# Converting the output projection's weights later, beside the gated block of batch 0, and spreading the other weight conversions over more of the attention

## The chip, the cores and the metric

The program runs on one core of a Trainium2 chip. The metric is the device time of one execution in microseconds (us). A core has five instruction streams: PE (matrix products), DVE and ACT (elementwise work and copies out of the accumulators), POOL (elementwise, slower), and SP, which here only issues DMA transfers. ACT issues DMA transfers too. Each stream runs its instructions strictly in its written order.

## The reference

Three stages, in float32 accuracy; batch 2, 8 heads, 768 positions, 64 values per head:

```python
# 1 attention, only between positions whose 6 hash bits agree
mask   = bucket(q @ proj) == bucket(k @ proj)
attn   = softmax(where(mask, q @ k.T / 8, -1e9));   x = attn @ v      # x: [2, 768, 512]
# 2 gated block ("MoE")
h = relu(x @ w_in);  u, v = h[..., :512], h[..., 512:]
v = w_spatial @ layernorm(v) + b_spatial            # mixes positions
x = (u * v) @ w_out
# 3 channel MLP
x = x + relu(layernorm(x) * g @ w_ch1) @ w_ch2      # 512 -> 2048 -> 512
```

The weights `w_in` (halves u and v, 512x512 each), `w_out` (512x512), `w_ch1` and `w_ch2` arrive as float64 values, that is as pairs of 32-bit words.

## The kernel before

**Products.** Each float32 operand is split into a high part of few bits and the remainder (`split_hi`, `split_lo`), and a product is three passes (high by high, high by low, low by high) of matrix instructions. So each weight tile exists as two halves, "hi" and "lo".

**Stages.** Attention runs in 96 steps: 2 batches x 8 heads x 2 groups x 3 query tiles of 128 rows (`attn_step`, line 876). A step makes scores (`sc`), their masked maximum (`x <- sc`, DVE), the exponentials (`x <- x`, ACT), their transposes on PE (`pt`), the copies of these out of the accumulators (`e <- pt`, shared between DVE and ACT), and once per head the product with v (`po`). Names carry batch, head, group and tile: `sc_1_2_0_1` is batch 1, head 2, group 0, tile 1. From step 60 (`M0`) on, the gated block of batch 0 (`moe1`, line 1007) is mixed in between the steps; that of batch 1 follows the attention, and the channel MLP follows it. In the gated block `pv_b_t_1` is the product of position tile t with the weight's v half, `pv_b_t_0` with its u half; `xT <- pv` (ACT) is the relu of the u half, `vr <- pv` (ACT) that of the v half; `act_x` is the split input, `vn` the normalized v, `w_sp` the split spatial weight.

**Converting a weight piece.** `conversions` (line 973) lists twelve pieces, four each of `out`, `v`, `u`. A piece has four parts (`converted`, line 942): a load of 512 KB of 64-bit words issued on ACT (`f64_*`), one ACT operation and five DVE operations on the two words (`f64c_*`), a join on POOL, and the split (hi by ACT, lo by POOL) into the weight tile. Once a whole weight is converted, it is stored to DRAM in one DMA of 2 MB issued on ACT (`kept`, line 966; `ws_out`, `ws_v`, `ws_u`); the copies that batch 1 needs, and `w_out` for both batches, are loaded back later by SP. `CONV_AT` (line 521) gives the attention step of each piece, and `CONV_D` the steps by which its parts stand off. `w_out` is converted first, in the buffer that later holds the normalized v (tag "vn"). The pieces of `w_ch1` and `w_ch2` (`f64_w1_*`, `f64_w2_*`) are converted in the same way in the later stages. The buffers of the loaded words and of the conversion's results are rings of two.

**What sets the order.** The kernel first records all operations as jobs (class `Plan`, line 170), so that every instruction carries line 494 in the profile. A list scheduler (`run`, line 296) then writes each engine's order: with modelled durations it takes, on the engine that is free first, the ready job with the earliest due time. Due times come from a pass backwards (`latest`, line 397); the two alternate and the best order is kept (`settle`). `opened` (line 317) holds a job back: until the matrix work recorded 60 jobs earlier has started, and until 20 us (`EARLY`) before its due time. So a changed place, size or buffer of one job may move instructions of every engine, also in stages that the change doesn't touch.

**SP's work in the attention.** For each head SP loads `k`, `q`, `v` and moves the split pieces into place: `qs <- q`, `ks <- k` and the mask rows `qs <- m`, `ks <- m`. The scores of a head wait for these.

Of the kernel before, what the change touches and what calls it, by code (L numbers as in the profile page):

```python
# [9 lines left out]
F32 = mybir.dt.float32  # L10
F32R = mybir.dt.float32r
# [7 lines left out]
P = 128  # L19
# [10 lines left out]
class View:  # L30


    def __init__(self, base, steps, box, dims, dtype):
        self.base, self.steps, self.box, self.dims, self.dtype = base, steps, box, dims, dtype
# [125 lines left out]
def cells(x):  # L160

    if isinstance(x, View):
        return x.columns
    n = 1
    for d in x.shape[1:]:
        n *= d
    return n


class Plan:  # L170
# [14 lines left out]
    RATE = {"load": 300e3, "move": 195e3, "store": 200e3}  # L185

    def __init__(self, tc):
        self.tc, self.jobs, self.pools, self.part, self.behind = tc, [], [], 0, None
        for name, key in (("tensor", "PE"), ("vector", "DVE"), ("scalar", "ACT"), ("gpsimd", "POOL"), ("sync", "SP")):
            setattr(self, name, Engine(self, key))  # L190

    def add(self, engine, op, args, kw):
        writes = [kw["out"] if "out" in kw else args[0]]
        rest = [*(args if "out" in kw else args[1:]), *(x for k, x in kw.items() if k not in ("out", "accum_out"))]
        if "accum_out" in kw:
            writes.append(kw["accum_out"])
        reads = [x for x in rest if isinstance(x, View)]
        views = [(x, True) for x in writes if isinstance(x, View)] + [(x, False) for x in reads]
        prev = self.jobs[-1] if self.jobs else None
        if (  # L200
            engine == "PE"
            and prev is not None
            and prev.engine == "PE"
            and prev.part == self.part
            and not prev.closed
            and prev.out is writes[0].base
            and prev.kind == (op, cells(writes[0]), writes[0].rows)
            and len(prev.calls) < (12 if cells(writes[0]) == 384 and op == "matmul" and reads[0].dtype == F32 else self.RUN)
        ):
            job = prev  # L210
        else:
            job = Job(len(self.jobs), engine, self.part)
            self.jobs.append(job)
            if engine == "PE":
                job.out, job.kind = writes[0].base, (op, cells(writes[0]), writes[0].rows)
        if self.behind:
            job.after.add(self.behind)
        busy, lag = self.cost(engine, op, writes, [x for x in rest if hasattr(x, "dtype")], kw, job)
        job.calls.append((op, args, kw))
        job.busy, job.lag = job.busy + busy, lag  # L220
        for x, w in views:
            for j, box, w2 in x.base.uses:
                if (w or w2) and j is not job and all(a < d and c < b for (a, b), (c, d) in zip(box, x.place)):
                    job.after.add(j)
            x.base.uses.append((job, x.place, w))
        return None
# [69 lines left out]
    def run(self, late=None):  # L296
# [12 lines left out]
        parts = {e: {} for e in engines}  # L309
# [5 lines left out]
        reached, when = [-1], [0.0]  # L315

        def opened(j):
            i = bisect_left(reached, j.at - self.LOOK)
            if i == len(reached):
                return None  # L320
            bulk = self.BULK if j.engine == "ACT" and j.bytes > 200000 else 0.0
            return max(when[i], bulk, late[j] - self.EARLY) if late else max(when[i], bulk)

        def done(j):
            stack = [j]
# [22 lines left out]
        while todo:  # L348
# [21 lines left out]
            j = min((j for j in c if ready[j] <= t + 1e-9), key=rank)  # L370
# [129 lines left out]
def attn_moe_kernel(ctx: ExitStack, tc: tile.TileContext, qT, kT, v, proj, w_in, w_spT, b_sp, w_out, g_ln, w1, w2, out):  # L500
# [3 lines left out]
    nc = plan = Plan(tc)  # L504
# [4 lines left out]
    w_in, w_out, w1, w2 = (  # L509
        w.bitcast(U32).rearrange("(k p) (f t) -> p k f t", p=P, t=2) for w in (w_in, w_out, w1, w2)  # L510
    )
    HF = DFF // 2
    DFF2 = w1.shape[2]
    NQT = S // P
    NKT = S // P
# [2 lines left out]
    CB0 = 2  # L518
    VB = (((0, 1, 2), (3, 4, 5)), ((0, 1), (2, 3, 4), (5,)))
    CB = 2  # L520
    CONV_AT = (5, 9, 14, 19, 24, 29, 34, 39, 44, 49, 53, 57)
    CONV_D = (-1, 0, 3, 3)
    QA = 3
    QB = 2
# [15 lines left out]
    KFT = DM // P  # L540
# [9 lines left out]
    def split_hi_v(dst, src):  # L550
        nc.scalar.activation(dst, src, AF.Copy)
# [4 lines left out]
    def split_lo(dst, src, hi):  # L556
        nc.gpsimd.tensor_tensor(dst, src, hi.bitcast(F32), op=ALU.subtract)
# [3 lines left out]
    def stage_f64(src, nm):  # L561
        a, n = src.shape[1], src.shape[2]
        st = pools["conv"].tile([P, a, n, 2], U32, tag="f64", name=f"f64_{nm}")
        nc.scalar.dma_start(out=st, in_=src)
        return st

    def words_f64(st, nm):

        a, n = st.shape[1], st.shape[2]
        lo, hi = st[:, :, :, 0], st[:, :, :, 1]  # L570
        c = pools["conv"].tile([P, a, n], U32, tag="f64c", name=f"f64c_{nm}")
        cf = c.bitcast(F32)
        nc.scalar.activation(cf, hi.bitcast(F32), AF.Abs)
        nc.vector.tensor_scalar(cf, cf, F64_MIN, F64_MAX, op0=ALU.max, op1=ALU.min)
        nc.vector.tensor_scalar(c, c, 3, 0x3FFFFFFF, op0=ALU.logical_shift_left, op1=ALU.bitwise_and)
        nc.vector.scalar_tensor_tensor(hi, hi, 0xC0000000, c, op0=ALU.bitwise_and, op1=ALU.bitwise_or)
        nc.vector.tensor_scalar(c, hi, 0xFF800000, None, op0=ALU.bitwise_and)
        nc.vector.scalar_tensor_tensor(cf, lo, 2.0**-52, cf, op0=ALU.mult, op1=ALU.mult)
        return hi.bitcast(F32), cf

    def join_f64(tf, cf):
        nc.gpsimd.tensor_tensor(cf, tf, cf, op=ALU.add)
        return cf

    def split_f64(dst_hi, dst_lo, tf):
        split_hi_v(dst_hi, tf)
        split_lo(dst_lo, tf, dst_hi)
# [20 lines left out]
    for a, own in enumerate((slice(0, D), slice(D, P))):  # L608
        for i, sign in enumerate((1.0, -1.0, 1.0)):
            at = a * HROW + i * NB  # L610
# [17 lines left out]
    dram = Pool(plan, "dram", space=bass.MemoryType.DRAM)  # L628
# [21 lines left out]
    mp = Pool(plan, "mp", 2, side="right", till=2)  # L650
# [287 lines left out]
    w_split = {}  # L938
    wp = {}
    moe_w = []  # L940

    def converted(src, dst, nm, after=None):

        d = {}

        def stage():
            d["st"] = stage_f64(src, nm)

        def words():
            d["tc"] = words_f64(d["st"], nm)  # L950

        def join():
            d["f"] = join_f64(*d["tc"])

        def finish():
            to = dst()
            split_f64(to[:, 0], to[:, 1], d["f"])
            if after:
                after(to)

        return stage, words, join, finish

    def kept(key, shape, to):
        w_split[key] = dram.tile(shape, F32, tag=f"ws_{key}", name=f"ws_{key}")
        nc.scalar.dma_start(out=w_split[key], in_=to.bitcast(F32))

    def moe_tile(key, b):
        pool = mp if len(moe_w) % 2 else keep
        wp[key, b] = pool.tile([P, 2, KFT, HF], F32R, tag="w", name=f"w_{key}_{b}", bufs=1)
        moe_w.append(wp[key, b])  # L970
        return wp[key, b]

    def conversions():

        res = []
        for key, src, at in (("out", w_out, 0), ("v", w_in, HF), ("u", w_in, 0)):
            for k in range(KFT):

                def dst(key=key, k=k):
                    if k == 0:  # L980
                        if key == "out":
                            wp[key] = mp.tile([P, 2, NKT, HF], F32R, tag="vn", name="w_out", bufs=1)
                        else:
                            wp[key] = moe_tile(key, 0)
                    return wp[key][:, :, k : k + 1]

                def after(to, key=key):
                    kept(key, [P, 2, KFT, HF], wp.pop(key)[:, :, :KFT])

                src_k = src[:, k : k + 1, at : at + HF]  # L990
                res.append(converted(src_k, dst, f"{key}_{k}", after if k == KFT - 1 else None))
        return res

    def reload(key, b):
# [148 lines left out]
    for _ in range(WARM2):  # L1143
        nc.tensor.transpose(warm, ident, ident)
    head_prep3(0, 0)
    convs = conversions()
    conv_steps = {}
    for at, stages in zip(CONV_AT, convs):
        for delay, e in zip(CONV_D, stages):
# [3 lines left out]
    for i in range(-1 - QA, NT + PO + 3):  # L1153
        attn_step(i)
        for e in pair_steps.get(i, ()):
            e()
        if i == 2:
            nc.sync.dma_start(out=b_sb, in_=b_sp.rearrange("(n p) -> p n", p=P))
        for e in conv_steps.get(i, ()):
            e()  # L1160
        if i == M0:
            m0 = moe1(0, ps_b, "b")
        if m0 is not None:
            while n0 < (i - M0 + 1) * 24 / (NT - M0):
                next(m0, None)
                n0 += 1
# [199 lines left out]
```

## Time and profile before

| | us |
|---|---|
| three runs | 665.03, 667.38, 668.51 |
| median | 667.38 |
| the profiled execution | 669.14 |
| its span on the core | 666.8 |
| PE busy in it | 651.5 |
| DVE, ACT, POOL busy | 430.3, 302.1, 198.3 |
| chain of work that ended last: PE, DVE, DMA | 87%, 7%, 3% |
| 2 MB stores issued on ACT at | 163.35 (w_out), 198.86 (w_v), 267.2 (w_u) |

"Busy" is the time in which an engine had an instruction running, out of the stretch named. Matrix instructions overlap each other and their ends are modelled, so that PE can read 100% and still run closer or wider. "Idle before" with an arrow names the instruction that ended a wait. A start is counted from the span's start. The attention of batch 0 and the beginning of batch 1 fill 10 to 155 us; the gated block of batch 0 lies beside the rest of the attention up to about 300; the gated block of batch 1 and the channel MLP follow.

### The profile page before, as it was taken

The page shows a single profiled execution, that of the slowest core. Times are in us where ns is not written, and L with a number is a line of the kernel's source. Part 1 is how long each engine was busy: PE and PEld are TensorE (multiplying, and loading weights), DVE is VectorE, ACT ScalarE, POOL GpSimd, SP SyncE. Part 2 cuts the span into 40 slices and gives each one's busy share as a digit, 9 for nine tenths or more (in the row PEclk, how much of TensorE's full clock was granted, in tenths as well). Part 3 has the DMA queues.
Part 4 walks back from the last instruction along what each step waited for, and adds up shares of the span by engine and source line. Part 5 has one row for each costly group of instructions (what it writes and reads, how often), then busy time and mean ns, then how long its engine had stood idle before and what let it go on. Part 6 is the DMA issues. An engine that isn't in the chain of part 4 may idle for free.

```text
span 666.8 us, 9374 instructions
## 1 busy us (share of the span) xinstructions
PE 651.5 (98%) x3376; PEld 510.2 (77%) x3376; DVE 430.3 (65%) x804; ACT 302.1 (45%) x581; POOL 198.3 (30%) x184
## 2 busy tenths in 40 slices
PE   7999999989999999999899999999999999999997
PEld 5776767767777777877688888888888888888886
DVE  5699779998657544443899695788862358622122
ACT  5788877776556545433364343432321133311110
POOL 2234424446325311100324433054450044510000
PEclk8999999999999999999899999999999999999999
DMA  6776775755539442906343441722210222200031
GB/s 167 187 190 168 190 162 154 220 134 179 146 97 336 102 105 71 327 27 227 129 151 121 144 132 47 284 95 87 84 51 1 64 85 87 81 1 16 1 111 63
DMA packets 47413, 83.72 MB, mean 126 GB/s; under 512 B 5676, under 2 KB 32136, under 8 KB 46344
## 3 DMA queue, kind: packets, MB, share of 16 engines
q1 hardware_dynamic: 34104, 53.64, 28.3%
q10 hardware_dynamic: 13264, 29.50, 13.2%
q8 instruction: 27, 0.44, 0.3%
q14 instruction: 18, 0.15, 0.1%
HBM read 51.42 MB, written 12.58 MB: 96 GB/s over the span
## 4 chain that ended last, share of the span: by engine, by line
PE 87%; DVE 7%; DMA 3%; issue 1%; ACT 1%; POOL 0%; SPq 0%; ACTq 0%; DVEq 0%; POOLq 0%
PE pc L494 20%; PE acc L494 20%; PE pv L494 8%; PE po L494 8%; PE sc L494 8%; PE pg L494 8%; PE pt L494 7%; PE py L494 5%; DVE x L494 2%; DMA f_w<-in_w 1%; DVE f64c_u L494 1%; PE pm L494 1%; PE ptr_g L494 1%; PE px_c L494 1%; DMA qs<-m 1%
## 5 line engine op out<-in xcount | busy, mean ns | idle before, releaser
L494 PE MATMUL acc<-w2t,ch 128*128 128x512 f32 x576 | 141.8, 393 | 0.0
L494 PE MATMUL pc<-xh,w1t 128*128 128x512 f32 x576 | 141.8, 394 | 0.0
L494 PEld LDWEIGHTS pc<-xh,w1t 128*128 128x128 f32 x576 | 108.0, 188 | 24.7
L494 PEld LDWEIGHTS acc<-w2t,ch 128*128 128x128 f32 x576 | 108.0, 188 | 24.5
L494 ACT ACTIVATE x<-x,nb 128x768 f32<-128x768 f32 x96 | 89.7, 935 | 29.9 <-DVE x L494 27.9
L494 DVE TENSOR_SCALAR_CACHE_REDUCE x<-sc 128x768 f32<-128x768 f32 x96 | 90.9, 952 | 17.8 <-PE sc L494 12.0
L494 DVE SCALAR_TENSOR_TENSOR ch<-pc,ch 128x512 fp32r<-128x512 f32 x48 | 33.1, 690 | 106.5 <-ACT ch L494 106.4
L494 PE MATMUL sc<-ks,qs 128*128 128x512 f32 (+3 forms) x384 | 94.9, 367 | 6.9 <-DVE x L494 3.6
L494 ACT ACTIVATE ch<-pc 128x512 fp32r<-128x512 f32 x48 | 28.7, 598 | 146.1 <-PE pc L494 146.0
L494 PE MATMUL pt<-ident,x 128*128 128x128 f32 x576 | 82.6, 276 | 0.9 <-DVE m L494 0.6
L494 PEld LDWEIGHTS sc<-ks,qs 128*128 128x128 f32 (+1 forms) x384 | 64.3, 194 | 21.7 <-DVE x L494 5.7
L494 POOL TENSOR_TENSOR f64c_w<-f_w,f64c_w 128x512 f32<-128x512 f32 x32 | 44.6, 1395 | 114.6 <-DVE f64c_w L494 95.0
L494 PEld LDWEIGHTS pt<-ident,x 128*128 128x128 f32 x576 | 68.0, 142 | 13.3 <-ACT e L494 4.1
L494 ACT ACTIVATE e<-pt 128x384 f32<-128x384 f32 x120 | 55.8, 484 | 26.5 <-PE pt L494 25.8
L494 PE MATMUL po<-e,vv 128*64 128x384 f32 x384 | 65.5, 490 | 0.0
L494 DVE COPY e<-pt 128x384 f32<-128x384 f32 x72 | 39.6, 552 | 17.9 <-PE pt L494 17.6
L494 PEld LDWEIGHTS po<-e,vv 128*64 128x64 f32 x384 | 26.2, 137 | 31.3 <-issue 30.1
L494 PE MATMUL pg<-vn,w_sp 128*128 128x512 f32 x180 | 45.0, 399 | 0.0
L494 PE MATMUL pv<-w_u,act_x 128*128 128x512 f32 x144 | 36.3, 400 | 2.3 <-ACT xT L494 2.2
L494 PEld LDWEIGHTS pg<-vn,w_sp 128*128 128x128 f32 x180 | 33.0, 188 | 7.1
L494 DVE TENSOR_SCALAR f64c_w<-f64c_w 128x512 f32<-128x512 f32 x64 | 32.6, 511 | 7.2 <-ACT f64c_w L494 6.5
L494 PE MATMUL pv<-w_v,act_x 128*128 128x512 f32 x144 | 37.1, 406 | 0.0
(132 smaller groups left out, 777.5 us busy)
## 6 DMA issues: line engine op xcount, KB each, us to landing
f_w<-in_w ACTq DMA_DIRECT2D x32, 512.0 KB
ks<-k SPq DMA_DIRECT2D x45, 192.0 KB
qs<-q SPq DMA_DIRECT2D x31, 192.0 KB
wst_sp<-in_w_spT SPq DMA_DIRECT2D x12, 384.0 KB
w_out<-ws_out SPq DMA_DIRECT2D x2, 2048.0 KB
vv<-in_v SPq DMA_DIRECT2D x16, 192.0 KB
ot<-y_dram SPq DMA_DIRECT2D x12, 256.0 KB
qs<-q SPq DMA_DIRECT2D x31, 96.0 KB
```

The source lines that it names most:

```text
L494: getattr(getattr(nc, engine[j.engine]), op)(*map(live, args), **{k: live(x) for k, x in kw.items()})
```

## The change

The order of the weights becomes v, u, out. The attention steps of the pieces become wider apart and later. A new flag `soon`, set while the conversions are recorded, takes their jobs out of the rule that holds a job until 20 us before its due time. The pieces of `w_out` no longer share the buffer "vn": hi and lo of a piece go into buffers of the spatial weight (tags `sp0`, two buffers, and `sp1`, one), and each is stored alone, 256 KB, so that `w_out` leaves in eight stores. `w_v` and `w_u` are still stored in one DMA of 2 MB each. No arithmetic is added or removed.

```diff
@@ -213,6 +213,7 @@
+        job.soon = self.soon
@@ -319,7 +320,7 @@
             if i == len(reached):
                 return None
             bulk = self.BULK if j.engine == "ACT" and j.bytes > 200000 else 0.0
-            return max(when[i], bulk, late[j] - self.EARLY) if late else max(when[i], bulk)
+            return max(when[i], bulk, late[j] - self.EARLY) if late and not j.soon else max(when[i], bulk)
 
         def done(j):
             stack = [j]
@@ -518,7 +519,7 @@
-    CONV_AT = (5, 9, 14, 19, 24, 29, 34, 39, 44, 49, 53, 57)
+    CONV_AT = (5, 11, 18, 24, 31, 37, 44, 50, 58, 62, 66, 70)
@@ -954,15 +955,10 @@
 
         def finish():
             to = dst()
-            split_f64(to[:, 0], to[:, 1], d["f"])
-            if after:
-                after(to)
+            split_f64(to[0], to[1], d["f"].rearrange("p a n -> p (a n)"))
+            after(to)
 
         return stage, words, join, finish
-
-    def kept(key, shape, to):
-        w_split[key] = dram.tile(shape, F32, tag=f"ws_{key}", name=f"ws_{key}")
-        nc.scalar.dma_start(out=w_split[key], in_=to.bitcast(F32))
 
     def moe_tile(key, b):
         pool = mp if len(moe_w) % 2 else keep
@@ -973,22 +969,29 @@
     def conversions():
 
         res = []
-        for key, src, at in (("out", w_out, 0), ("v", w_in, HF), ("u", w_in, 0)):
+        for key, src, at in (("v", w_in, HF), ("u", w_in, 0), ("out", w_out, 0)):
+            w_split[key] = dram.tile([P, 2, KFT, HF], F32, tag=f"ws_{key}", name=f"ws_{key}")
             for k in range(KFT):
 
                 def dst(key=key, k=k):
+                    if key == "out":
+                        parts = [
+                            mp.tile([P, NKT * P], F32R, tag=f"sp{i}", name=f"w_out_{k}_{i}", bufs=2 - i) for i in range(2)
+                        ]
+                        return [x[:, :HF] for x in parts]
                     if k == 0:
-                        if key == "out":
-                            wp[key] = mp.tile([P, 2, NKT, HF], F32R, tag="vn", name="w_out", bufs=1)
-                        else:
-                            wp[key] = moe_tile(key, 0)
-                    return wp[key][:, :, k : k + 1]
-
-                def after(to, key=key):
-                    kept(key, [P, 2, KFT, HF], wp.pop(key)[:, :, :KFT])
+                        wp[key] = moe_tile(key, 0)
+                    return [wp[key][:, i, k] for i in range(2)]
+
+                def after(to, key=key, k=k):
+                    if key == "out":
+                        for i in range(2):
+                            nc.scalar.dma_start(out=w_split[key][:, i, k], in_=to[i].bitcast(F32))
+                    elif k == KFT - 1:
+                        nc.scalar.dma_start(out=w_split[key], in_=wp.pop(key).bitcast(F32))
 
                 src_k = src[:, k : k + 1, at : at + HF]
-                res.append(converted(src_k, dst, f"{key}_{k}", after if k == KFT - 1 else None))
+                res.append(converted(src_k, dst, f"{key}_{k}", after))
         return res
 
     def reload(key, b):
@@ -1156,8 +1159,10 @@
             e()
         if i == 2:
             nc.sync.dma_start(out=b_sb, in_=b_sp.rearrange("(n p) -> p n", p=P))
+        plan.soon = True
         for e in conv_steps.get(i, ()):
             e()
+        plan.soon = False
         if i == M0:
             m0 = moe1(0, ps_b, "b")
         if m0 is not None:
```

The scheduler carries this further. Three places matter below. In each the name of an instruction is "written <- read".

First, ACT where the attention has ended and the gated block of batch 1 begins. Before (`f64_w1_1` is a load that ACT issues, `xT_1...<-pv_1_1_0` the relu of tile 1's u half):

```order
L494 DMA f64_w2_0_3576<-in_w2 128x1024
L494 ACTIVATE f64c_w1_0_3584<-f64_w1_0_3526 128x512
L494 ACTIVATE act_x1_3_3621<-xT_1_1858 128x512
L494 ACTIVATE xT_1_1858<-pv_1_0_0_3568 128x4x128
L494 ACTIVATE vr_1_2_3637<-pv_1_2_1_3569 128x512
L494 ACTIVATE f64c_w2_0_3640<-f64_w2_0_3576 128x512
L494 DMA f64_w1_1_3659<-in_w1 128x4x256
L494 ACTIVATE xT_1_1858<-pv_1_1_0_3627 128x4x128
L494 ACTIVATE act_x1_4_3665<-xT_1_1858 128x512
L494 ACTIVATE w1t_0_3678<-f64c_w1_0_3584 128x512
L494 ACTIVATE w_sp_early_3680<-wst_sp1_1_3578 128x768
```

Now:

```order
L495 ACTIVATE f64c_w1_0_3582<-f64_w1_0_3538 128x512
L495 ACTIVATE act_x1_3_3627<-xT_1_1842 128x512
L495 ACTIVATE xT_1_1842<-pv_1_0_0_3584 128x4x128
L495 DMA f64_w2_0_3635<-in_w2 128x1024
L495 ACTIVATE vr_1_2_3644<-pv_1_2_1_3585 128x512
L495 ACTIVATE w_sp_early_3663<-wst_sp1_1_3592 128x768
L495 ACTIVATE act_x1_4_3676<-xT_1_1842 128x512
L495 ACTIVATE xT_1_1842<-pv_1_1_0_3637 128x4x128
L495 ACTIVATE f64c_w2_0_3700<-f64_w2_0_3635 128x512
L495 ACTIVATE vn_1_3703<-vr_1_0_3568 128x512
L495 ACTIVATE xc_0_0_3536<-xc_0_0_3536,r0_c0_3666 128x512
L495 ACTIVATE vr_1_3_3716<-pv_1_3_1_3669 128x512
```

The load of `f64_w1_1` and the relu of `pv_1_1_0` have changed places: the load stood right ahead of the relu, and now it stands ten rows behind it, below the last row shown. The relu stands three rows behind `vr_1_2` in both, and `f64_w2_0`'s first ACT operation, which stood ahead of the relu, now stands behind it and ahead of `vr_1_3`.

Second, DVE around the first steps of head 1 of batch 1. Before (`f64c_u` and `f64_u` belong to the conversion of the u weight):

```order
L494 TENSOR_SCALAR f64c_u_1_1739<-f64c_u_1_1739 128x512
L494 TENSOR_SCALAR x_1_1_1_0_1838,nb_1_1_1_0_1837<-sc_1_1_1_0_1795 128x768
L494 COPY e_1_1_0_1798<-pt_1_1_0_0_1_1789 128x3x128
L494 TENSOR_SCALAR x_1_1_1_1_1847,nb_1_1_1_1_1846<-sc_1_1_1_1_1805 128x768
L494 TENSOR_SCALAR f64c_u_1_1739<-f64c_u_1_1739 128x512
L494 COPY e_1_1_0_1798<-pt_1_1_0_1_1_1818 128x3x128
L494 SCALAR_TENSOR_TENSOR f64_u_1_1665<-f64_u_1_1665,f64c_u_1_1739 128x512
L494 TENSOR_SCALAR f64c_u_2_1840<-f64c_u_2_1840 128x512
L494 COPY xT_1_1858<-po_1_0_1822 64x384
L494 TENSOR_SCALAR f64c_u_1_1739<-f64_u_1_1665 128x512
L494 TENSOR_SCALAR f64c_u_2_1840<-f64c_u_2_1840 128x512
L494 TENSOR_SCALAR x_1_1_1_2_1882,nb_1_1_1_2_1881<-sc_1_1_1_2_1860 128x768
```

Now:

```order
L495 TENSOR_SCALAR x_1_1_0_2_1781,nb_1_1_0_2_1780<-sc_1_1_0_2_1760 128x768
L495 SCALAR_TENSOR_TENSOR q2_1_1_1624<-q2_1_1_1624 128x768
L495 TENSOR_SCALAR x_1_1_1_0_1807,nb_1_1_1_0_1806<-sc_1_1_1_0_1785 128x768
L495 COPY e_1_1_0_1783<-pt_1_1_0_0_1_1776 128x3x128
L495 TENSOR_SCALAR x_1_1_1_1_1833,nb_1_1_1_1_1832<-sc_1_1_1_1_1803 128x768
L495 COPY e_1_1_0_1783<-pt_1_1_0_1_1_1798 128x3x128
L495 COPY xT_1_1842<-po_1_0_1813 64x384
L495 TENSOR_SCALAR x_1_1_1_2_1864,nb_1_1_1_2_1863<-sc_1_1_1_2_1845 128x768
L495 COPY e_1_1_0_1783<-pt_1_1_0_2_1_1851 128x3x128
L495 COPY e_1_1_1_1872<-pt_1_1_1_0_1_1866 128x3x128
L495 TENSOR_SCALAR x_1_2_0_0_1896,nb_1_2_0_0_1895<-sc_1_2_0_0_1878 128x768
```

The conversions of the u weight are gone from this place. They stand earlier; the pieces of `w_out` follow from head 2 of batch 1 on.

Third, ACT at the end of head 4 of batch 0. Before:

```order
L494 ACTIVATE e_0_4_0_901<-pt_0_4_0_2_0_961 128x3x128
L494 ACTIVATE e_0_4_1_995<-pt_0_4_1_0_0_982 128x3x128
L494 ACTIVATE e_0_4_1_995<-pt_0_4_1_0_1_988 128x3x128
L494 ACTIVATE x_0_4_1_2_993,z_sum_0_208<-x_0_4_1_2_993,nb_0_4_1_2_992 128x768
L494 ACTIVATE f64c_v_1_1028<-f64_v_1_958 128x512
```

Now:

```order
L495 ACTIVATE e_0_4_1_984<-pt_0_4_1_0_1_980 128x3x128
L495 ACTIVATE e_0_4_1_984<-pt_0_4_1_1_0_986 128x3x128
L495 DMA ws_v_1016<-w_v_0_599 128x4096
L495 ACTIVATE x_0_4_1_2_1011,z_sum_0_208<-x_0_4_1_2_1011,nb_0_4_1_2_1010 128x768
L495 ACTIVATE x_0_5_0_0_1031,z_sum_0_208<-x_0_5_0_0_1031,nb_0_5_0_0_1030 128x768
```

The 2 MB store of `w_v` has come here; before, it stood in batch 1, beside the gated block. In the same way that of `w_u` now stands ahead of the first exponential of batch 1's head 1.

## Rows read from the trace of the kernel before

**Rows 1.** First page: span, and PE's busy time.

```profile
span 666.8 us, 9374 instructions
...
PE 651.5 (98%) x3376; PEld 510.2 (77%) x3376; DVE 430.3 (65%) x804; ACT 302.1 (45%) x581; POOL 198.3 (30%) x184
```

**Rows 2.** Busy us by stretch: PE, PEld, DVE, ACT, POOL; PE clock; DMA; GB/s.

```profile
325.75:328.09 2.34, 0.16 (x1) 0.00 (x1) 2.34 (x4) 0.65 (x2) 2.23 (x2) 1.00 0.02 3
328.09:333.00 4.91, 4.91 (x15) 3.89 (x16) 3.79 (x9) 2.28 (x5) 1.70 (x2) 0.65 0.33 107
```

**Rows 3.** Timeline of POOL; start, us, instruction, idle before and releaser.

```profile
325.03 1.90 POOL L494 TENSOR_TENSOR f64c_w<-f_w,f64c_w 128x512 f32<-128x512 f32 x1 [3.80 <-DVE f64c_w L494]
```

**Rows 4.** Timeline of ACT at the same place.

```profile
326.95 0.39 ACTq L494 DMA_DIRECT2D f_w<-in_w  x1
327.44 0.60 ACT L494 ACTIVATE xT<-pv 128x512 f32<-128x512 f32 x1 [4.00 <-POOL f64c_w L494]
```

**Rows 5.** Timeline of PE at the same place.

```profile
328.09 1.75 PE L494 MATMUL pv<-w_u,act_x 128*128 128x512 f32 x6 [2.18 <-ACT xT L494]
```

**Rows 6.** Busy us by stretch over the attention, columns as in rows 2.

```profile
20.00:60.00 40.00, 39.06 (x268) 27.78 (x267) 35.13 (x71) 32.74 (x72) 14.33 (x14) 1.00 0.69 177
60.00:100.00 40.00, 39.37 (x266) 28.56 (x266) 32.49 (x71) 32.99 (x72) 14.81 (x15) 1.00 0.73 178
100.00:130.00 30.00, 29.25 (x199) 20.81 (x196) 27.72 (x56) 24.18 (x52) 12.53 (x13) 1.00 0.69 189
130.00:160.00 30.00, 28.24 (x185) 19.86 (x183) 29.81 (x56) 21.33 (x44) 15.75 (x15) 1.00 0.62 162
160.00:200.00 40.00, 39.66 (x227) 31.19 (x226) 24.37 (x54) 21.61 (x43) 15.03 (x14) 1.00 0.44 124
```

**Rows 7.** Timeline of DVE, the same form of instruction twice.

```profile
143.01 0.42 DVE L494 TENSOR_SCALAR f64c_u<-f64c_u 128x512 uint32<-128x512 uint32 x1
...
145.67 1.50 DVE L494 TENSOR_SCALAR f64c_u<-f64c_u 128x512 uint32<-128x512 uint32 x1
```

**Rows 8.** Timeline of POOL beside it.

```profile
145.50 2.80 POOL L494 TENSOR_TENSOR act_x<-xT,act_x 128x512 fp32r<-128x512 f32 x2 [4.91 <-ACT act_x L494]
```

**Rows 9.** Timeline of PE behind it.

```profile
148.23 0.98 PE L494 MATMUL sc<-ks,qs 128*128 128x512 f32 x4 [1.54 <-DVE x L494]
```

**Rows 10.** Waits of PE, 20 to 160 us: waited for, total, times, longest.

```profile
PE sc L494 <- DMA qs<-m: 0.7, 1, 0.7
```

**Rows 11.** Timeline of SP with no store beside it.

```profile
130.41 1.30 SPq L494 DMA_DIRECT2D qs<-q  x2
131.76 0.79 SPq L494 DMA_DIRECT2D qs<-m  x1
132.65 1.12 SPq L494 DMA_DIRECT2D ks<-k  x2
```

**Rows 12.** Timeline of SP right behind the store of w_out.

```profile
165.73 2.10 SPq L494 DMA_DIRECT2D qs<-q  x2
167.87 1.52 SPq L494 DMA_DIRECT2D qs<-m  x1
169.50 1.66 SPq L494 DMA_DIRECT2D ks<-k  x2
```

**Rows 13.** Instructions by form, DVE, 0 to 340 us: count, busy, mean ns.

```profile
L494 DVE SCALAR_TENSOR_TENSOR f64c_out<-f_out,f64c_out 128x512 f32<-128x512 uint32 x4 | 3.9, 963 | 0.1
...
L494 DVE TENSOR_SCALAR f64c_out<-f64c_out 128x512 uint32<-128x512 uint32 x4 | 2.9, 726 | 0.1
L494 DVE SCALAR_TENSOR_TENSOR f_out<-f_out,f64c_out 128x512 uint32<-128x512 uint32 x4 | 2.8, 692 | 0.0
...
L494 DVE TENSOR_SCALAR f64c_out<-f64c_out 128x512 f32<-128x512 f32 x4 | 1.9, 475 | 1.7 <-ACT f64c_out L494 1.7
...
L494 DVE TENSOR_SCALAR f64c_out<-f_out 128x512 uint32<-128x512 uint32 x4 | 1.7, 426 | 0.1
```

**Rows 14.** Timeline of DVE, the last two additions.

```profile
663.17 0.76 DVE L494 TENSOR_TENSOR ot<-acc,ot 128x256 f32<-128x256 f32 x2 [0.67 <-PE acc L494]
```

More of the change, by code (lines that the diff above doesn't have):

```diff
@@ L187, in __init__ @@
     def __init__(self, tc):
-        self.tc, self.jobs, self.pools, self.part, self.behind = tc, [], [], 0, None
+        self.tc, self.jobs, self.pools, self.part, self.behind, self.soon = tc, [], [], 0, None, False
         for name, key in (("tensor", "PE"), ("vector", "DVE"), ("scalar", "ACT"), ("gpsimd", "POOL"), ("sync", "SP")):
```

## The prediction

> **What bounds the kernel now.** The first page is read first: PE works 651.5 of 666.8 us [rows 1]. A change that leaves the arithmetic alone can only touch the other 15 us, or the spacing within. So the next view is busy time by stretch, to find where PE is not full. The reader is to see two places. One is the attention from 20 to 160 us, where PE stands idle 0.94, 0.63, 0.75 and 1.76 us in the four stretches, while DVE is busy 88, 81, 92 and 99% of them; from 160 to 200 us DVE falls to 61% and PE idles 0.34 us [rows 6]. So PE's small losses grow with DVE's load there. The other is the passage from attention to the gated block of batch 1, near 326 us. The timelines of the engines in these two places then say which instruction comes last.
>
> At 328.09 PE waits 2.18 us for a relu of ACT [rows 5]. ACT could not do it because a load issued by ACT stands ahead of it and waited for a buffer until POOL's join ended at 325.03 + 1.90 = 326.93 [rows 3]; the load goes at 326.95 and the relu at 327.44, after 4.00 us idle [rows 4]. Behind this pause the granted clock is 0.65 for 4.91 us [rows 2], a mixture of its two levels, 1.2 and 2.4 GHz, after a stretch at full clock in which PE worked only 0.16 of 2.34 us. The slow stretch costs 4.91 x (1 - 0.65) = 1.7 us beside the pause, together 3.9.
>
> **The change, part by part.** The sum is made against the profiled execution, 669.14 us, which is span 666.8 and 2.3 around it; it lies 1.8 above the median of the three runs, 667.38, and the answer is brought down by that at the end.
>
> *The passage near 326 us.* The load that blocked the relu now stands ten rows behind it. The relu of tile 1's u half then waits only for its own product, so the 2.18 us and the slow clock behind them should go: -3.9. What is late next: the copy `vr_1_3` now stands behind the first ACT operation on `f64_w2_0`, which needs a load of 512 KB, and behind `xc_0_0`, which needs a small chain of DVE and POOL. In the new order the POOL step of that chain stands ahead of the join, where it stood behind it. I count 0.7 us for a wait of PE there: the product that needs the accumulator copied by `vr_1_3` comes after 24 more matrix instructions, some 5 us, which is about what the chain takes. The bounds: nothing, or all of the old price again and 1 more. Taken: -3.9 + 0.7 = -3.2, range -3.9 to +1.
>
> *DVE from 130 to 160 us.* The u conversions leave this place, as the second pair of order rows shows. One of them carried PE's longest wait here: the same form of TENSOR_SCALAR took 0.42 us at 143.01 and 1.50 at 145.67 [rows 7], while POOL ran `act_x` from 145.50 for 2.80 us [rows 8]; the maximum for the scores stood behind it and PE idled 1.54 us [rows 9]. With DVE at the load of 160 to 200, PE's idle time per us there (0.34 in 40) makes 0.25 in these 30 us instead of 1.76: -1.5, range -1.76 to 0.
>
> *DVE from 20 to 130 us.* Heads 1 to 7 of batch 0 carried 3, 7, 7, 3, 10, 1 and 8 conversion operations in DVE's order, now 2, 7, 7, 4, 5, 5 and 5: 39 against 35. That is no relief worth a number: 0, bounds +1 and, if all idle time there went, -(0.94 + 0.63 + 0.75) = -2.3.
>
> *The pieces of w_out beside the gated block.* Five DVE operations of 0.963, 0.726, 0.692, 0.475 and 0.426 us make 3.28 a piece [rows 13], four pieces 13.1. In 160 to 200 us DVE was busy 24.4 of 40 [rows 6]; with these it is 37.5, or 94%, as from 100 to 130 us, where PE idled 0.75 in 30. That is 1.0 in 40 against 0.34: +0.6, range 0 to the rate of 130 to 160 (1.76 in 30, so 2.35 in 40), +2.0. Their stores are small, stand on ACT behind each piece's own hi copy or POOL's lo, and ACT has 18 of 40 us free there; nothing is added for them.
>
> *The two 2 MB stores.* They move from the gated block of batch 0, where PE has other products to run when scores are late, into the attention of batch 0 and the first head of batch 1, where it has few. Beside such a store SP's issues lengthen: 1.30, 0.79 and 1.12 us for five transfers [rows 11] become 2.10, 1.52 and 1.66 [rows 12], 2.1 us more. DMA is already the last to arrive once, 0.7 us for mask rows [rows 10], so the slack in front of the scores is not large everywhere. If none of the 2.1 us were hidden, PE would also fall to the slow clock behind each pause, 1.7 by the passage above: 3.8 a store, 7.6 for both. If SP is as far ahead as it mostly is (one wait worth naming in 140 us), nothing. I take 1.0, near the one measured wait, range 0 to 7.6. The Trainium skill, "DMA: Bandwidth & Descriptors", section "Issuing engines are not separate DMA queues", says that transfers issued by different engines run on the same 16 DMA engines and interleave; the trace agrees, with SP's 2.1 us beside a store of ACT, and by this rule alone moving a store to ACT's idle time would hide nothing from SP.
>
> *The end.* The last tile's two half additions of 0.38 us each [rows 14] become, in the new order, one whole one with one whole store: a last addition longer by some 0.3 (a second half of 0.38 against a whole of about twice that), less what the second issue cost. Taken +0.2, range 0 to +0.4.
>
> The sum is -3.2 - 1.5 + 0 + 0.6 + 1.0 + 0.2 = -2.9, so 669.1 - 2.9 = 666.2 for the profiled execution, and less 1.8 against the median: **664.5 us**, or 0.4% under 667.38.
>
> **The rivals.** First, *the passage gives nothing*: the wait moves from the relu to `vr_1_3`. For it: that copy stands behind two instructions that wait for others. Against it: the load for one of them is issued earlier than in before, and PE has 24 matrix instructions in hand. It gives 664.5 + 3.2 = 667.7, no change. The same time comes out if the conversions don't get easier in any stretch.
>
> Second, *the stores win*: SP's loads for the heads behind each 2 MB store come late and PE pauses in full, with the slow clock behind it, 7.6 instead of 1.0: 671.1. From a price of 3.9 for both the change is slower than before, from 7.2 on by over 0.5%. For it: rows 12, and DVE at 81% and more, so that PE is never far ahead. Against it: no wait of PE for a DMA is longer than 0.7 us in the attention, though some ten heads are loaded there beside conversion loads of 512 KB.
>
> Third, *more than the named waits goes*: the small idle times from 20 to 130 us go too (-2.3) and the stores cost nothing (-1.0): 661.2. For it: a more even spread lets each engine's order loosen. Against it: the first heads have nearly the same conversion operations as before.
>
> Fourth, *DVE and POOL meet beside the gated block*. POOL was busy 15.0 of 40 us from 160 to 200 [rows 6] and gets the joins and lo halves of four pieces on top. If more TENSOR_SCALARs take 1.50 instead of 0.42, say six of twelve, DVE has 6.5 us more, 44 of 40, and becomes the bound: +4 less the 0.6 counted, 667.9. The Trainium skill, "SBUF — State Buffer", section "Who interferes with whom", says that DVE in its two-port modes and GpSimd shut each other out of a shared pair of ports for a whole instruction; the one clear case in this trace, 1.50 against 0.42 beside POOL, agrees. Against it: the mean of 0.726 and 0.475 for the same forms in rows 13 holds such meetings already.
>
> **How the numbers follow.** Runs of this kernel tell no change apart under some 0.5%, 3.3 us. The forecast gets 0.48, and its own range is 662.8 to 666.3, so that a little under half of it lies beyond -0.5%. The first rival gets 0.16, the second 0.12, the third 0.16, the fourth 0.08. Faster: 0.48 x 0.47 + 0.16 and a little of the others, 0.40. Slower: most of the second and a little of the first and fourth, 0.13. The rest is 0.47 within 0.5%. The range reaches from just under the third rival's 661.2 to between the fourth and the second: 660.5 to 669.0.
>
> **What would show it.** In the new profile: no wait of PE for `xT` near 325 us and the clock at 1.00 there (the first term); no wait of PE for DVE over 1 us between 130 and 160, with DVE near 70% (the second); PE idle some 1.0 from 160 to 200 with DVE over 90% (the third); SP's issues behind the new places of the stores at 2.1 and 1.5 us, and no wait of PE for `qs` or `ks` over 0.7 (the fourth). A wait `sc <- DMA` of two us with a clock below 1.00 behind it would make the prediction wrong on the slow side; PE idle under 0.4 us in each of the four stretches of the attention, on the fast side.

## The result

The changed kernel takes 674.88 us in the median of four runs (673.89 to 676.22), the kernel before 667.5: a ratio of 1.0102, 95% interval 1.0079 to 1.0126. It is slower by 7.4 us. Forecast were 664.5, with 660.5 to 669.0 as the range; the time lies outside, on the side of the second rival (671.1, chance 0.12), and beyond it. One execution of a kernel below, and one of the kernel before beside it, ran at clock 0.65 throughout (922 us); ratios and intervals leave these two out.

The profiled execution took 675.69 us with a span of 673.7, 6.9 more than before. The waits of PE in the attention show where. Columns are: who waited for whom, us in total, times, longest.

```profile
PE sc L495 <- issue: 4.5, 1, 4.5
PE sc L495 <- DMA qs<-q: 3.8, 1, 3.8
PE pt L495 <- DVE xT L495: 0.8, 1, 0.8
PE sc L495 <- DVE x L495: 0.7, 2, 0.5
```

Before there was no wait here over 1.54 us. Now there are two of about 4 us, and both stand in front of scores. The timeline of PE shows their places (the second line is a product that runs at once behind the first pause):

```profile
86.40 1.62 PE L495 MATMUL sc<-ks,qs 128*128 128x512 f32 x4 [4.50 <-issue]
87.95 4.59 PE L495 MATMUL po<-e,vv 128*64 128x384 f32 x14
...
156.96 1.48 PE L495 MATMUL sc<-ks,qs 128*128 128x512 f32 x4 [3.77 <-DMA qs<-q]
```

The 4.50 us are put down to "issue", that is, to nothing that the profile could name. The instruction is the first product with the second half of head 5's `qs`. The timelines of ACT and SP around it point to the cause:

```profile
77.25 0.35 ACTq L495 DMA_DIRECT2D ws_v<-w_v  x1
```

```profile
76.86 1.44 SPq L495 DMA_DIRECT2D qs<-q  x2
78.35 1.61 SPq L495 DMA_DIRECT2D qs<-m  x1
80.06 2.84 SPq L495 DMA_DIRECT2D ks<-k  x2
83.07 3.50 SPq L495 DMA_DIRECT2D qs<-q  x2
86.67 0.62 SPq L495 DMA_DIRECT2D ks<-k  x1
```

ACT issues the 2 MB store at 77.25. The product is served by three transfers of SP. SP issues the first two in the stretch from 76.86 to 78.30 and the third, the mask rows, at 78.35, so around and just behind the store. Everything that SP issues until 86.6 us takes longer, up to 2.7 times as long: the pairs take 1.44, 2.84 and 3.50 us (1.30 for `qs` and 1.12 for `ks` with no store beside them, [rows 11]). By the packet records of the trace the store's packets run from 79.20 to 85.62; PE goes on at 86.40, when the store is through. The second pause begins the same way; here a load of 512 KB follows the store at once:

```profile
141.37 0.33 ACTq L495 DMA_DIRECT2D ws_u<-w_u  x1
141.75 0.46 ACTq L495 DMA_DIRECT2D f_out<-in_w_out  x1
```

```profile
146.68 2.48 SPq L495 DMA_DIRECT2D ks<-k  x1
149.25 2.13 SPq L495 DMA_DIRECT2D qs<-q  x2
151.69 0.80 SPq L495 DMA_DIRECT2D ks<-m  x1
```

The pair at 149.25 is what the product at 156.96 needs. Here the way from the store to the pause is longer: the store's last packet ends at 151.42, 5.5 us before PE goes on, and what moves in between is mostly what SP itself has in hand, beside the rest of the load (from 152 to 155 us 103 to 126 KB in each us from SP's queue, and 86 falling to 12 from ACT's). That this comes of the store is not seen in these rows; it rests on the runs below, in which the wait goes with the store. The busy shares by stretch (columns as in rows 2) show how full the DMA engines were, and what came behind the two waits:

```profile
78.00:81.90 3.90, 3.90 (x30) 2.75 (x28) 3.90 (x9) 3.50 (x8) 2.69 (x2) 1.00 0.98 332
81.90:86.40 4.50, 0.00 (x1) 0.03 (x1) 1.37 (x3) 2.20 (x5) 0.00 (x0) 0.89 0.97 325
86.40:91.00 4.60, 4.60 (x14) 2.42 (x16) 2.79 (x6) 1.03 (x2) 0.00 (x0) 0.50 0.57 129
91.00:95.00 4.00, 4.00 (x23) 1.95 (x20) 1.50 (x4) 0.79 (x2) 1.30 (x1) 0.84 0.00 2
...
153.20:156.96 3.76, 0.00 (x1) 0.04 (x1) 0.95 (x4) 1.40 (x3) 0.36 (x1) 1.00 0.77 153
156.96:162.00 5.04, 5.04 (x25) 4.66 (x25) 2.58 (x7) 2.07 (x4) 0.00 (x0) 0.66 0.74 192
```

The DMA engines are 97 to 98% busy at 325 GB/s and more until PE may go on at 86.40, and 57% at 129 GB/s after it; during the second pause they are 77% busy at 153 GB/s. Of PE's two levels, 1.2 and 2.4 GHz, the lower one alone (0.50) stands behind the first pause and then a mixture (0.84); behind the second it is a mixture, 0.66. Worked out as in the prediction this costs 4.6 x 0.50 + 4.0 x 0.16 = 2.9 us, and 5.04 x 0.34 = 1.7.

Busy time over the stretches that answer to [rows 6], and over the passage:

```profile
20.00:60.00 40.00, 38.43 (x259) 27.03 (x259) 33.02 (x67) 31.50 (x70) 14.18 (x13) 1.00 0.68 177
60.00:100.00 40.00, 34.83 (x218) 24.29 (x215) 27.71 (x58) 26.30 (x58) 13.41 (x12) 0.91 0.67 191
100.00:130.00 30.00, 29.82 (x199) 21.39 (x198) 25.53 (x55) 23.64 (x52) 9.19 (x9) 1.00 0.68 166
130.00:160.00 30.00, 26.20 (x171) 18.85 (x169) 22.17 (x44) 19.22 (x42) 11.02 (x11) 0.95 0.81 222
160.00:200.00 40.00, 40.00 (x234) 30.06 (x234) 35.19 (x68) 24.34 (x49) 18.95 (x18) 0.99 0.51 145
...
300.00:340.00 40.00, 39.57 (x200) 30.48 (x199) 22.78 (x56) 16.81 (x33) 5.06 (x5) 1.00 0.41 142
```

From 160 to 200 us PE is full now, though DVE is busy 35.2 of 40. The passage has become whole as well: 39.57 of 40 from 300 to 340 where it was 37.82, at clock 1.00; there is one wait of 0.43 us for `vr_1_3`.

| from the two traces, after less before | us | predicted |
|---|---|---|
| two waits for `qs`, 4.50 + 3.77 | +8.3 | } +1.0 |
| slow clock behind them, 2.9 + 1.7 | +4.6 | } (0 to 7.6) |
| passage near 326 us, 0.4 in place of 3.9 | -3.5 | -3.2 |
| DVE from 130 to 160, no wait for it left | -1.7 | -1.5 |
| pieces of w_out beside the gated block, idle 0.00 against 0.34 | -0.3 | +0.6 |
| other idle time, 0 to 130 us (-1.0, +0.6, 0.0, -0.6) | -1.0 | 0 |
| behind 340 us (a wait of 0.2 for DVE; the end isn't told apart) | +0.2 | +0.2 |
| sum | +6.6 | -2.9 |
| measured between the spans | +6.9 | |

Of the other idle time, the 1.0 of the first 20 us can't be put down to the change: with the instructions in the very same order (the first run below) PE idles 5.15 us there, against 3.98 here and 4.99 before. From 20 to 60 us these two traces differ by 0.8. Terms of about 1 us and less are therefore not told from what varies between executions.

### The profile page after: what moved, and what is told of

It is laid out like the page before. It is cut to its first block, busy times and chain, and to the rows that moved or that the text cites. A ratio compares the mean times of both kernels' runs of the same rounds, so it can differ in the third digit from the quotient of the medians.

```text
span 673.7 us, 9371 instructions
## 1 busy us (share of the span) xinstructions
PE 654.6 (97%) x3376; PEld 511.5 (76%) x3376; DVE 429.4 (64%) x804; ACT 302.8 (45%) x581; POOL 197.5 (29%) x184
## 3 DMA queue, kind: packets, MB, share of 16 engines
q10 hardware_dynamic: 14144, 29.50, 13.8%
## 4 chain that ended last, share of the span: by engine, by line
PE 84%; DVE 5%; DMA 5%; ACT 3%; issue 1%; SPq 0%; POOL 0%; DVEq 0%; ACTq 0%
PE pc L495 19%; PE acc L495 19%; PE po L495 9%; PE sc L495 8%; PE pt L495 8%; PE pg L495 7%; PE pv L495 7%; PE py L495 5%; DVE x L495 1%; DMA f_w<-in_w 1%; ACT x L495 1%; DMA qs<-q 1%; DMA f_v<-in_w_in 1%; DMA y_dram<-xc 1%; PE ptr_g L495 1%
## 5 line engine op out<-in xcount | busy, mean ns | idle before, releaser
L495 PE MATMUL sc<-ks,qs 128*128 128x512 f32 (+3 forms) x384 | 96.9, 375 | 11.7 <-issue 4.5
L495 PEld LDWEIGHTS sc<-ks,qs 128*128 128x128 f32 (+1 forms) x384 | 67.2, 199 | 25.3 <-issue 7.8
L495 PE MATMUL po<-e,vv 128*64 128x384 f32 x384 | 67.6, 503 | 0.0
L495 DVE TENSOR_SCALAR f64c_w<-f64c_w 128x512 f32<-128x512 f32 (+1 forms) x64 | 34.7, 544 | 20.5 <-ACT f64c_w L495 20.0
L495 ACT ACTIVATE f64c_w<-f_w 128x512 f32<-128x512 f32 x32 | 21.4, 669 | 32.6 <-DMA f_w<-in_w 32.3
```

Of the source, the lines that this page charges most:

```text
L495: getattr(getattr(nc, engine[j.engine]), op)(*map(live, args), **{k: live(x) for k, x in kw.items()})
```

## The experiments

**The stores' size of run.** Every instruction in the changed kernel's place; only the copies in DRAM are padded, so that a store, and later the load back, goes in pieces of 2 KB and not in runs of 16 KB:

```diff
-w_split[key] = dram.tile([P, 2, KFT, HF], F32, ...)
+w_split[key] = dram.tile([P, 2, KFT, HF + 16], F32, ...)[:, :, :, :HF]
```

> The changed kernel with every instruction in the same place; only the rows of the three weight copies in DRAM are padded from 512 to 528 values, so that the 2 MB stores go in pieces of 2 KB instead of 16 KB runs. Theory A (the two DMA queues of ACT and SP take turns packet by packet, so that SP's packets of about 1.5 KB wait behind store packets that took 0.63 us each): SP's loads land within 3 to 4 us beside the store, the waits of 4.5 us at 86 and 3.8 us at 157 us shrink below 1.5 us each, and the time falls to 664 to 668 us. Theory B (what counts is the 2 MB in flight; the store has to be through before SP's transfers land): both waits stay within 1 us of what they were, time 673 to 677 us.

Measured: 673.66 us, ratio to before 1.0101 (1.007 to 1.0133). The page counts 15,936 packets on ACT's queue in place of 14,144, which is the two stores in 1,024 pieces each and not in 128. The longest waits of PE from 20 to 160 us:

```profile
PE sc L495 <- issue: 2.7, 1, 2.7
PE sc L495 <- DMA qs<-q: 2.4, 1, 2.4
```

The two waits became 2.7 and 2.4, 3.2 us shorter together, and the slow clock stayed (0.91 and 0.94 from 60 to 100 and 130 to 160; behind the shorter first pause 5.18 us at 0.50, 5 us at 0.87). Neither theory has it: A wanted under 1.5 each and 664 to 668 us, B wanted them within 1 us of what they were. The time is B's, the waits lie between the two. So smaller pieces alone don't free SP's transfers. Counted from the packet records, ACT's queue moved 342 to 375 KB in each us from 80 to 85, and SP's 15 to 36; in the changed kernel it was 246 to 442 against 0 to 97.

**The stores back beside the gated block.**

```diff
+plan.soon = False
 nc.scalar.dma_start(out=w_split[key], in_=wp.pop(key).bitcast(F32))
+plan.soon = True
```

> The changed kernel, but the two 2 MB stores of w_v and w_u are held back as in the kernel before (the flag is off for these two jobs alone); they stand beside the gated block again, all else of the change stays. If the early stores made the whole loss: no wait of PE for qs, clock 1.00 from 80 to 170 us, and the two waits (4.5 and 3.8 us) with the slow clock behind them (about 4.6 us) are gone, 12.9 us less than the changed kernel's 674.9, about 662; but the scheduler has put the load of f64_w1_1 ahead of the relu of pv_1_1_0 again, so up to 3.9 us come back there: 662 to 666 us. If the late landings come from the conversions' new order or pieces instead, it stays above 670 us.

Measured: 663.67 us, ratio 0.994 (0.9909 to 0.9972). With only the two early stores undone in the kernel's text, the change is a gain of 0.6%; the scheduler's order is again another one. Waits from 20 to 160 us, and the timeline of PE at the passage:

```profile
PE sc L495 <- DVE x L495: 1.3, 4, 0.5
PE pt L495 <- DVE m L495: 0.8, 1, 0.8
PE sc L495 <- PE pt L495: 0.5, 1, 0.5
```

```profile
324.76 1.65 PE L495 MATMUL pv<-w_u,act_x 128*128 128x512 f32 x6 [1.67 <-ACT xT L495]
```

No wait for `qs` is left; the clock is 1.00 from 20 us on. At the passage the load of `f64_w1_1` stands ahead of the relu again, and 1.67 us of waiting for `xT` have come back, as expected; this time without a slow clock.

**No flag at all.** `plan.soon = True` becomes `False`; stores and conversions are held back by their due times again.

> The changed kernel without the flag: order v, u, out, the wider steps and the pieces in the spatial weight's buffers stay, but every conversion job is held back by its due time again, and so are the stores. Early stores as the cause: about 662 to 664 us, since here the load of f64_w1_1 stands behind the relu and no wait of 2 us for xT is expected. Wider steps or pieces as the cause: above 670 us.

Measured: 665.71 us, ratio 0.9974 (0.9957 to 0.9991): below the 670 us of wider steps or pieces as the cause, though above the 662 to 664 expected. So the order v, u, out, the wider steps and the pieces in the spatial weight's buffers do no harm to the time as a whole. In the attention from 20 to 160 us PE waits 0.2 us in all; but DVE is busy 37.15 of 40 from 160 to 200, and PE loses 1.45 there and 2.13 from 200 to 300:

```profile
160.00:200.00 40.00, 38.55 (x215) 29.64 (x214) 37.15 (x73) 25.64 (x51) 24.85 (x21) 1.00 0.56 159
200.00:300.00 100.00, 97.87 (x551) 75.53 (x550) 52.50 (x107) 47.65 (x93) 25.45 (x21) 0.98 0.53 169
```

**The kernel before, with early stores.** The flag itself is added as in the change; then:

```diff
+plan.soon = True
 nc.scalar.dma_start(out=w_split[key], in_=to.bitcast(F32))
+plan.soon = False
```

> The kernel before with one thing of the change: the three 2 MB stores are not held back by their due times and so are issued as soon as their weight is whole; w_out's store then stands at head 4 of batch 0, w_v's at the beginning of batch 1, w_u's at head 2 of batch 1. If early stores cost by themselves: two or three waits of PE for qs or ks of 2 to 5 us each behind them with a clock below 1.00 after each, 675 to 682 us. If it takes the conversions' new order for it: within 3 us of before, 665 to 670 us.

Measured: 668.27 us, ratio 1.0012 (0.999 to 1.0034): no change, where waits and 675 to 682 us were expected. The waits are there all the same:

```profile
PE sc L495 <- DMA qs<-q: 6.5, 4, 3.2
```

```profile
85.15 0.95 PE L495 MATMUL sc<-ks,qs 128*128 128x512 f32 x4 [3.23 <-DMA qs<-q]
...
142.36 0.94 PE L495 MATMUL sc<-ks,qs 128*128 128x512 f32 x4 [1.39 <-DMA qs<-q]
```

The store of `w_out` goes at 74.96 and PE pauses 3.23 us up to 85.15; that of `w_v` goes at 133.45 and it pauses 1.39 up to 142.36. That is 4.6 of the 6.5 us; the other two waits, 1.17 and 0.73 us, stand ahead of any store. Behind the store of `w_u`, at 169.99 beside the gated block, PE waits for no DMA. Of the two or three waits of 2 to 5 us expected only one is there. From 60 to 100 us the clock is 0.96. But the scheduler, given the stores earlier, also wrote another order elsewhere: the wait of 1.54 us for DVE is gone, and at the passage PE has no wait and is busy 40.00 of 40 from 300 to 340. So loss and gain cancel in the time, as far as these rows tell. By the time alone early stores would cost nothing by themselves; the waits say that they do, but less here than in the changed kernel (4.6 us of pauses against 8.3).

**The passage alone.** In the kernel before, the second piece of w_ch1 is recorded later, so that its load stands 18 rows behind the relu:

```diff
-(5, lambda: w1_piece(1)),
+(10, lambda: w1_piece(1)),
```

> The kernel before with the second piece of w_ch1 recorded later in the gated block of batch 1, so that its load stands on ACT 18 rows behind the relu of pv_1_1_0 instead of right ahead of it; the attention's conversions and the stores stay. If the passage near 326 us cost 3.9 us (2.2 of waiting, 1.7 of slow clock): no wait for xT there, and 663 to 665 us beside 667.5 to 668. If the wait only moves to another instruction: no change, 667 to 669.

Measured: 664.33 us, ratio 0.9917 (0.9889 to 0.9946). The same kernel was run once more for its profile:

> The kernel of the fifth run once more, for its profile. If the passage near 326 us was the gain: no wait of PE for xT there, PE busy 40.0 of 40 us from 300 to 340 at clock 1.00, where the kernel before has 37.8 at 0.96; the stretches from 20 to 160 us as before, within 1 us. If the gain came from elsewhere (a new order in the attention): the passage still waits over 1 us.

Measured: 664.55 us, ratio 0.9953 (0.9926 to 0.998). By stretch:

```profile
20.00:60.00 40.00, 39.09 (x262) 27.32 (x262) 32.22 (x65) 30.55 (x69) 11.33 (x12) 1.00 0.62 164
60.00:100.00 40.00, 38.98 (x264) 28.31 (x262) 34.75 (x75) 33.71 (x74) 17.55 (x17) 1.00 0.70 180
100.00:130.00 30.00, 30.00 (x209) 21.71 (x203) 26.12 (x54) 24.68 (x54) 14.25 (x14) 1.00 0.71 191
130.00:160.00 30.00, 29.82 (x188) 21.15 (x187) 27.54 (x56) 20.57 (x44) 12.32 (x12) 1.00 0.65 175
...
300.00:340.00 40.00, 39.27 (x188) 29.41 (x187) 27.41 (x60) 19.83 (x37) 8.86 (x7) 1.00 0.54 185
```

From 300 to 340 PE is busy 39.27 at clock 1.00, not the 40.0 expected, and waits for `xT` no more; one wait of 0.6 for `xc` is new. Against before that is 1.45 us less idle and 1.6 of clock (0.96 over 40 us), 3.1 together. But PE also idles 2.1 us from 20 to 160 where it was 4.1, more than the 1 us allowed for, and 1.6 behind 340 where it was nothing. So the fall of 4.2 to 5.4 us against the runs beside it is not the passage's alone.

**Both together.** Late stores, and the load behind the relu.

> Late stores as in the second run (663.7 us, with a wait of 1.7 us for xT near 326), and the load of f64_w1_1 behind the relu as well. If the two gains add: 661 to 662.5 us, no wait for xT. If the wait near 326 us is replaced by another one: 663 to 665.

Measured: 663.2 us, ratio 0.9902 (0.9877 to 0.9928), against 0.994 for late stores alone: the intervals overlap. No wait for `xT` is left, but one of 1.4 us for `vn` stands behind 345 us that wasn't there. The wait was mostly replaced.

**The stores by pieces.** All three weights are stored as `w_out` is, 256 KB at a time when a piece is done; the flag stays on:

```diff
-if key == "out":
-    for i in range(2): nc.scalar.dma_start(out=w_split[key][:, i, k], ...)
-elif k == KFT - 1: nc.scalar.dma_start(out=w_split[key], ...)
+for i in range(2): nc.scalar.dma_start(out=w_split[key][:, i, k], ...)
```

> The changed kernel with the flag on all stores, but w_v and w_u are stored piece by piece as w_out is, 256 KB each and spread from head 2 to head 2 of the next batch, in rows of 2 KB. The bytes are the same and still cross the attention. If the harm is 2 MB in one go, in front of which SP's loads have to wait until it has passed: no wait of PE for a DMA over 1 us, 662 to 667 us. If any store of these bytes in the attention takes the loads' share: waits for qs or ks of 3 us and more in all, above 670 us.

Measured: 660.02 us (658.36 to 662.2), ratio 0.9851 (0.9809 to 0.9893): 1.5% faster than before, by the medians 2.2% faster than the changed kernel, and the best of all. The same 4 MB cross the attention, in sixteen stores, the last one issued at 136.79. PE's waits from 20 to 160 us are one line:

```profile
PE sc L495 <- DMA qs<-q: 0.8, 1, 0.8
```

```profile
73.43 1.34 SPq L495 DMA_DIRECT2D qs<-q  x2
74.82 0.89 SPq L495 DMA_DIRECT2D qs<-m  x1
```

SP issues at its usual pace beside them, 1.34 us for a pair where it was up to 3.50. The order of the instructions is another one too, and the passage has no wait here (PE 40.00 of 40 from 300 to 340), so that not all of the gain is the stores'. SP also issues the transfers for the second half of head 5 at 73.43, 3.4 us earlier than in the changed kernel, which gives them more slack. But the bytes as such did not do the harm; what is left is 2 MB in one go, with little slack behind it.

**Half the bytes in one go.** Only the hi halves are stored, 1 MB each.

> The changed kernel, storing only the hi half of w_v and w_u, 1 MB instead of 2 (batch 1 then computes with the hi half twice: the low half of these two weights is left out there). The store of w_v stays at head 4 of batch 0, that of w_u moves to head 2 of batch 1 beside the gated block. If SP's loads wait for the store's own running time, near 6 us for 2 MB: the wait of 4.5 us at 86 us falls by about 3, to 1 to 2 us, the one at 157 goes, 664 to 668 us. If the wait comes from SP's own place in order or from the conversion loads beside it: 4 us or more stay at 86 us and the time stays above 669.

Measured: 666.05 us, ratio 0.9944 (0.9919 to 0.9969). With `w_v`'s store again at 77.17 the wait behind it is 0.61 us:

```profile
83.18 0.50 PE L495 MATMUL sc<-ks,qs 76*128 76x512 f32 x1 [0.61 <-DMA qs<-m]
```

The wait at 157 is gone, and the store of `w_u`, now at 154.40, has none behind it; one more wait for a DMA, 1.55 us for `ks` at 36.30, stands ahead of any store. The 0.61 is less than the 1 to 2 expected, and it isn't a clean dose: the scheduler let SP issue this head's `qs` from 75.67 on, 1.2 us earlier than in the changed kernel, all three transfers ahead of the store. That place alone did not save them: the mask rows, issued at 77.02, serve the product only at 83.18, when the store of 1 MB ends (its last packet at 83.42). Counted from the store's issue PE goes on after 6.0 us, where it was 9.15 behind 2 MB. This speaks for the store's length; how the 3.9 us saved divide between the bytes and the place in SP's queue, this run doesn't tell.

## Why the prediction was wrong

**What bounds the kernel.** Right: PE's small waits, in the attention and at the passage. The prediction also named its own sign of being wrong on the slow side, a wait of scores for a DMA of two us with a slow clock behind it, and that is what the trace shows.

**The passage, and DVE from 130 to 160 us.** Both right in mechanism and size: -3.5 against -3.2 and -1.7 against -1.5, with no wait for `xT` or for DVE left. Even the wait that the prediction named as the next one, for `vr_1_3`, is there, at 0.43 against 0.7. Moving that one load alone gave 3.1 us at the passage, which agrees; that run's order changed elsewhere too.

**The pieces of w_out.** The cost of +0.6 was taken from DVE's load: 94% should have left PE 1.0 us idle, as from 100 to 130. DVE came to 35.2 of 40, not 37.5, and PE idled not at all. So DVE at 88% cost PE nothing here. (Without the flag, DVE at 93% did cost 1.45 us there, so it depends on the order.) The fourth rival falls with it: the three forms of TENSOR_SCALAR on a piece took 0.669, 0.577 and 0.417 us there, together 1.66 where it was 1.63 before. The -0.3 where +0.6 was forecast, and the -1.0 of other idle time, are luck on the fast side, of a size that varies between executions.

**The two 2 MB stores.** This is the step that failed. The term was taken at 1.0 with 7.6 as its top. Measured were 7.4 and 5.5, 12.9 together: beyond the top of the range. Two things were missed. First, the price was built from the length of SP's issues beside a store, but what makes PE wait is the landing and not the issue. In the kernel before no wait made the landing visible, since beside the gated block PE had other products to run. Yet its trace holds it. SP issues a pair and its mask rows from 165.73 [rows 12], and from 164 to 169 us the DMA view of that trace has packets of ACT's queue alone (columns: packets, MB, share of 16 engines):

```profile
q10 hardware_dynamic: 225, 1.84, 89.0%
```

The first packet of SP's queue starts at 169.64, and by the count of packets the pair and the mask rows have landed at 171.40, 5.7 us behind the first issue; their product starts at 171.81, so nothing waited. A transfer issued just behind the store can thus be about as late as the store is long (8.4 us from issue to last packet at the first store in the changed kernel), and that, less the slack, is the bound from above that should have stood there. Second, the value chosen, 1.0, was taken near a wait of 0.7 us [rows 10] that stood at another place, without a store beside it; it said that the slack was small and was read as a small price. The rule quoted there from the Trainium skill ("DMA: Bandwidth & Descriptors", section "Issuing engines are not separate DMA queues") pointed the right way: the transfers of ACT and SP run on the same engines and interleave. The trace now agrees that they share them, with DMA at 97% and SP's transfers late. But beside the store in the kernel before SP's queue got no packet in for 5 us, where the rule speaks of interleaving; how unevenly the two share is not in it and was measured here.

The second rival had the place, the mechanism and the sign right; its price of 7.6 was too low, and its chance of 0.12 rested on the waits of a kernel without such stores in the attention. That the harm comes of the 2 MB stores and not of the conversions' new places is shown by the runs with late stores and with pieces, with the reserve that the scheduler's order changed in both; in the run with the order kept, the waits changed with the size of the stores' pieces.

In the sums, the share of the forecast beyond -0.5% was taken as 0.47; 664.05 us cuts off 1.25 of the 3.5 us from 662.8 to 666.3, about a third, so that faster was given somewhat too much.

What stays open: why SP's transfers get so small a share beside the store. Pieces of 2 KB in place of runs of 16 KB shortened the two waits from 8.3 to 5.1 us but left the time almost as it was.

## What to carry to other kernels

A bulk transfer that is moved is priced by its running time at its new place, against the slack of every load issued behind it there; that nothing waited beside it at the old place says little, if the engine had other work at hand. The packet records at the old place, of when the other queue's transfers moved, say more. Store by pieces as they are finished: two stores of 2 MB cost 12.9 us here, and the same bytes in sixteen stores, in another order of the instructions, left one wait of 0.8. Where a scheduler writes the order, compare waits and not only times, since one edit brought 4.6 us of them and took away as much elsewhere.

## What the hardware showed

Beside the first 2 MB store from ACT's queue the DMA engines ran at 97 to 98% and 325 to 332 GB/s, and SP's issue of a pair of transfers took 3.50 us in place of 1.30. In the kernel before, SP's queue moved no packet for 5 us beside such a store, with three transfers issued in that time. A pause of PE by 4.50 us was followed by 4.6 us at clock 0.50 and 4 us at 0.84, one of 3.77 by 5 us at 0.66, one of 3.23 (the kernel before with early stores) by 4.85 at 0.65, one of 2.71 (small pieces) by 5.18 at 0.50 and 5 at 0.87, and one of 2.18, at the passage before, by 4.9 at 0.65. Pauses of 1.67 us, at the passage with late stores, and of 1.39 us, with early stores, were followed by none. Worked out as above, the slow stretches cost 1.7 to 3.2 us each, and not in step with the pause: 2.9 behind 4.50, 3.2 behind 2.71, 1.7 behind the other three.
